# Input transfers of 112 partitions, first weights two pieces an iteration, dummy rows cleared later

## The chip, the cores and the metric

The kernel runs on one core of one Trainium2 chip. The core has five engines with queues of their own: TensorE (PE), VectorE (DVE), ScalarE (ACT), GpSimd (POOL) and SyncE (SP). SP does no arithmetic here; it issues nearly all transfers, in the order in which the program gives them. The metric is the time of one execution on the device in microseconds (us); the time before is 335.15 us, the median of three runs.

## What is computed

A recurrence with a state per head (4 batches, 8 heads, 768 steps, head size 48) produces 3072 rows of 384 numbers, and each row then goes through one of eight experts.

```python
for t in range(S):                       # per batch and head
    cur = u * k[t] (outer) v[t]
    y[t] = r[t] @ (state + cur)
    state = w[t][:, None] * state + k[t] (outer) v[t]
x = y as rows [B * S, H * D]             # 3072 x 384
logits = x @ w_gate + modality_bias[modality_id]
e = argmax(logits); g = softmax(logits)[e]
out[row] = g * (relu(x[row] @ w1[e]) @ w2[e])
```

## The kernel before, in words

The recurrence is cut into 24 units (`NU`), six chunks of 128 steps for each of four batches. A unit's r, k and w come from one host array `rkw[n]` of 128 partitions by 1536 numbers (`LIN`): columns 0 to 511 are r, 512 to 1023 k, 1024 to 1535 w. The partitions are two halves of 64, one for each head of a pair; in a half 48 rows carry numbers, and the other 16 hold zeros in r and k and ones in w, the same in every unit. So partitions 112 to 127 are constant throughout. The unit's v is a second transfer of 128 by 384 (`loadv`).

One software pipeline of iterations i = -2 to 23 runs the units. In iteration i, stage a = i + 2 does the decay scans and scales keys and rows on DVE, stage m = i + 1 makes the products of the chunk, stage z = i finishes the outputs, and stages z - 1 and z - 2 turn them into expert rows and logits. POOL works one unit ahead of a: the products of decays (`decays`, L282), of r and k (`keys`, L287) and the inner decays (`within`, L299) are made for unit i + 3. `within` writes into the input tile itself, by multiplying its r and k columns by w columns.

The input tiles are four (`ins`, `NIN` = 4), used in turn. `load(n)` (L109) fills tile n mod 4. Before the loop units 0, 1 and 2 are issued; iteration -2 issues units 3 and 4; after that iteration i issues unit i + 6, in three pieces of 256 KB, each of which waits on SP until the tile's last reader in the iteration is done. The unit's first use is in iteration n - 3, three iterations behind its issue.

Two more kinds of transfers stand in the same SP queue during the loop. `fill(j)` (L231) clears 128 of the 512 dummy rows of the DRAM buffer `xs`, with 193 KB each, in iterations `FILL` to `FILL` + 3. `w_raw` (L269) brings the first expert's weights, whose number `e0` SP reads from the tile `e0i` at iteration `EARLY`, in 16 pieces of 192 KB: eight of w1 into `raw[0]`, then eight of w2 into `raw[1]`, one an iteration. The piece order in a matrix is 2, 3, ... 7, 0, 1, since piece 0 of both tiles serves as scratch for the routing's set-up (`mf`, `bt2`) until iteration 10.

Routing of the first ten units runs in iterations 11 to 14 behind the pipeline. From iteration 15 POOL scatters the rows of the first six units into `xs`, one an iteration (`scatter`, L724). At iteration 20 (`LOAD`) SP waits for those scatters and issues the load of the first block of rows (`blk_load(0)`, L751). DVE transposes it in iterations 22 and 23 (`blk_turn`, L770), ACT and POOL split the first w1 pieces in iterations 22 and 23 (`w_split`, L276 and L277), and behind iteration 23 PE begins the experts: seven blocks of up to 512 rows with matrix products in three parts (L792 up, L813 down).

Of the kernel before, what the change touches and what calls it, by code (L numbers as in the profile page):

```python
# [17 lines left out]
B, H, S, D = 4, 8, 768, 48  # L18
P = 128
# [6 lines left out]
FC = F // P  # L26
# [37 lines left out]
SCATTER = PART[0] + 3  # L64
NEAR = 6
DRAIN = {SCATTER + 2 + n: 1 for n in range(NEAR)}
EARLY = 6
FILL = 2
NPW = 3
LOAD = SCATTER + 1 + NEAR  # L70

# [2 lines left out]
def kernel(ctx: ExitStack, tc: tile.TileContext, rkw, vt, wf, cst, mid, wg, bias, w1, w2, out):  # L74
    nc = tc.nc
# [19 lines left out]
    NIN = 4  # L95
    ins = [pa.tile([P, LIN], F32, name=f"in{i}", bufs=1) for i in range(NIN)]
# [8 lines left out]
    def pt(n, tag, sh=(P, 512)):  # L105
        T[tag, n] = (bp["s"] if tag in ("pS0", "pS1") else ps).tile(list(sh), F32, tag=tag, name=f"{tag}_{n}")
        return T[tag, n]

    def load(n, cuts=((0, LIN),)):  # L109
        for c0, c1 in cuts:  # L110
            nc.sync.dma_start(out=ins[n % NIN][:, c0:c1], in_=rkw[n, :, c0:c1])

    def loadv(n):
        nc.sync.dma_start(out=wt(n, "v", [P, DM], 4), in_=vt[n * P:(n + 1) * P, :])

    load(0, ((1024, LIN), (512, 1024)))
    wm = cp.tile([P, 512], BF16, name="wm")
    nc.vector.memset(wm, 0.0)  # L120
    cs = cp.tile([P, NCST], F32, name="cs")
    nc.sync.dma_start(out=cs[:, 0:P], in_=cst[:, 0:P])
    load(0, ((0, 512),))
    act = cp.tile([1, 1], F32, name="act")
    nc.vector.memset(act, 0.0)
# [54 lines left out]
    def early():  # L180
        nc.sync.dma_start(out=bb, in_=bass.AP(bias.tensor, bias.offset, [[0, P], [1, 2 * E]]))
        nc.sync.dma_start(out=mi, in_=mid)
# [47 lines left out]
    def fill(j):  # L230
        nc.sync.dma_start(out=xs[DUMMY + j * P:DUMMY + j * P + P, :], in_=zt)  # L231
# [36 lines left out]
    def w_raw(e, k, part, cond=None, parts=2):  # L268
        n = FC // parts  # L269
        kw = {} if cond is None else {"cond": cond}  # L270
        nc.sync.dma_start(out=raw[k][:, part * n:part * n + n, :].rearrange("p f c -> p (f c)"),
                          in_=(w1, w2)[k][ds(e, 1), :, part * n * DM:(part + 1) * n * DM].rearrange("a p c -> (a p) c"), **kw)
# [41 lines left out]
    def ok(n):  # L314
        return 0 <= n < NU
# [238 lines left out]
    def route_a(c):  # L554

        n = PART[c]
        sh = [P, n, E]
        lg = rcol(FROM[c] * E, n, E)
        if c:
            clear(c)  # L560
        nc.vector.scalar_tensor_tensor(out=lg, in0=lg, scalar=-1.0, in1=biasT[:, units(c)], op0=ALU.mult, op1=ALU.subtract)
        mx = wt(c, "mx", [P, NMOST], 1)[:, 0:n]
        nc.vector.tensor_reduce(out=mx, in_=lg, axis=AX.X, op=ALU.min)
        nc.vector.tensor_tensor(out=rcol(C_RK, n, E + 1)[:, :, 1:E + 1], in0=lg, in1=mx[:, :, None].to_broadcast(sh), op=ALU.is_equal)
        yield
        eq, flat = rcol(C_RK, n, E + 1), lambda t: t[:, 0:n].rearrange("p a b -> p (a b)")
        nc.vector.tensor_tensor_scan(out=flat(seen), data0=flat(same), data1=rcol(C_RK, n * (E + 1)), initial=0.0, op0=ALU.mult, op1=ALU.max)
        oh = T["oh", c] = wt(c, "oh", [P, NMOST, E], 2, BF16)[:, 0:n]
        nc.vector.tensor_tensor(out=oh, in0=eq[:, :, 1:E + 1], in1=seen[:, 0:n, 0:E], op=ALU.is_gt)
        yield  # L570
        nc.vector.tensor_tensor(out=lg, in0=lg, in1=mx[:, :, None].to_broadcast(sh), op=ALU.subtract)
        if c:
            with nc.allow_low_precision("whole numbers up to 10"):
                nc.vector.tensor_reduce(out=ohs, in_=T["oh", 0].rearrange("p a b -> p b a"), axis=AX.X, op=ALU.add)
        nc.gpsimd.tensor_copy(out=T["xp", c][:, :, DM + 1:DM + 2].bitcast(I32), in_=tidi[:, units(c), None])
        yield
# [168 lines left out]
    def blk_load(q, at=None):  # L745
        at = q if at is None else at
        w = width(q)
        nj, rest = divmod(w, P)
        xq, xg = x_tiles(q)
        r = nc.sync.value_load(tab[0:1, 1, ds(at, 1)], min_val=0, max_val=DUMMY)  # L750
        ins = [nc.sync.dma_start(out=xq[SQ * g:SQ * g + SQ, 0:w // SQ],  # L751
                                 in_=xs[ds(r, w), QW * g:QW * g + QW].rearrange("(t p) c -> p t c", p=SQ)) for g in range(4)]
        ins.append(nc.sync.dma_start(out=xg[:, 0:nj], in_=xs[ds(r, nj * P), DM:XW].rearrange("(j p) c -> p j c", p=P)))
        if q == 0:
            for i in ins:
                tc.add_to_no_dep_group("x0", i.ins)
        if rest:
            nc.sync.dma_start(out=xg[0:rest, nj], in_=xs[ds(r + nj * P, rest), DM:XW])
# [125 lines left out]
    setup_m()  # L884
    keys(0)
    load(1, ((1024, LIN),))
    loadv(0)
    nc.sync.dma_start(out=cs[:, P:NCST], in_=cst[:, P:NCST])
# [5 lines left out]
    def drain(n):  # L894
        for _ in range(n):
            if pend:
                n = pend.pop(0)
                if n >= NEAR:
                    place(n, 1)
                scatter(n)  # L900

    def hook_b(c):
        route_b(c)
        pend.extend(range(FROM[c], FROM[c] + PART[c]))

    for i in range(-2, NU):
        if EARLY <= i < EARLY + 2 * FC:
            if i == EARLY:
                e0 = nc.sync.value_load(e0i[0:1, 0:1], min_val=0, max_val=E - 1)
            w_raw(e0, (i - EARLY) // FC, (i - EARLY + 2) % FC, parts=FC)  # L910
        if 1 <= i < 1 + len(SETUP):
            hooks.append(SETUP[i - 1])
        if FILL <= i < FILL + BW // P:
            fill(i - FILL)
        if i == PART[0] + 1:
            ra, tb = route_a(0), table(0)
            hooks.extend([lambda: next(ra), lambda: [*ra], lambda: hook_b(0), lambda: [*tb]])
        if i == NU - 1:
            prep.close()
        att_iter(i)  # L920
        if i >= -1 and ok(i + 3):
            loadv(i + 3)
        if i == -2:
            load(3)
        if i == 0:
            early()
        if ok(i + 2 + NIN):
            load(i + 2 + NIN, ((512, 1024), (1024, LIN), (0, 512)))
        drain(DRAIN.get(i, 0))
        if i == LOAD:  # L930
            blk_load(0)
# [291 lines left out]
```

## Time and profile before

| | |
|---|---|
| median of three runs | 335.15 us (334.73 to 335.19) |
| the profiled execution | 335.87 us, its span 334.1 us |
| mean granted TensorE clock | 0.994 |
| busy share PE, DVE, ACT, POOL | 97%, 71%, 62%, 48% |
| recurrence, first to last PE work of a unit | to 121.84 us of the span |
| bytes on SP's queue | 42.09 MB |

The profile describes one execution. The span goes from the first to the last instruction. A row of a timeline gives start, duration, engine, source line, operation, destination and source, and in brackets the idle time ahead of the instruction and what ended it; without brackets the engine had no idle time worth listing there. A busy PE is not a PE at its peak.

### The profile page before, as it was taken

How to read it: one execution, taken by the hardware profiler on the slowest of the kernel's cores; microseconds unless marked ns; L12 is line 12 of the kernel's file. 1: busy time of each engine (PE TensorE's matmuls, PEld its weight loads, DVE VectorE, ACT ScalarE, POOL GpSimd, SP SyncE). 2: the span in 40 equal slices, each digit the busy share in tenths (PEclk: the TensorE clock that was granted, in tenths of full speed). 3: DMA queues.
4: the chain of work that ended last, by engine and by line, in shares of the span. 5: the costliest groups of instructions: out<-in, count | busy, mean ns of one | idle time of the engine just before them, and what ended most of it. 6: DMA issues, size and time to landing. Idle time of an engine off the chain costs nothing.

```text
span 334.1 us, 10250 instructions
## 1 busy us (share of the span) xinstructions
PE 323.0 (97%) x3915; PEld 298.8 (89%) x3915; DVE 238.4 (71%) x510; ACT 206.2 (62%) x516; POOL 158.8 (48%) x194
## 2 busy tenths in 40 slices
PE   8989899999999999999999999999999999999993
PEld 3779899999898988899889999999999988999982
DVE  7899999999999886696458858858358445815510
ACT  2478388688879994461449556956956944614420
POOL 5889999999999179136751210210220220121021
PEclk9999799999999999999999999999999999999999
DMA  7998888888894601614964800440560663210001
GB/s 220 404 307 249 248 257 267 263 261 268 264 312 154 145 4 47 144 71 169 301 195 120 254 32 0 108 177 2 114 194 2 197 141 96 94 72 22 0 32 55
DMA packets 38735, 52.31 MB, mean 157 GB/s; under 512 B 19189, under 2 KB 26133, under 8 KB 38676
## 3 DMA queue, kind: packets, MB, share of 16 engines
q1 hardware_dynamic: 35572, 42.09, 42.9%
q0 software_dynamic: 3104, 9.47, 7.6%
q8 instruction: 33, 0.54, 0.7%
q14 instruction: 26, 0.21, 0.2%
HBM read 55.43 MB, written 11.88 MB: 202 GB/s over the span
## 4 chain that ended last, share of the span: by engine, by line
issue 40%; PE 20%; POOL 8%; POOLq 2%; ACT 1%; DVE 0%; ACTq 0%
PE pS_u L792 6%; POOL out L835 6%; PE pY_d L813 3%; PE pX_d L813 2%; POOL xs L724 2%; PE pY L466 2%; POOLq L1032 2%; PE pS L415 1%; PE pY L455 1%; PE pR_x L520 1%; PE pU L435 1%; PE pR_x L321 1%; ACT dV L356 0%; POOLq L835 0%; POOLq L1010 0%
## 5 line engine op out<-in xcount | busy, mean ns | idle before, releaser
L835 POOL DMA_INDIRECT out<-ot,xg x25 | 27.4, 1096 | 132.7 <-ACT ot L834 130.6
L797 DVE SCALAR_TENSOR_TENSOR hl<-pS_u,hh 128x512 fp32r<-128x512 f32 (+2 forms) x56 | 34.6, 619 | 62.5 <-ACT hh L796 62.3
L792 PE MATMUL pS_u<-xh,wh 128*128 128x512 f32 (+2 forms) x168 | 61.6, 367 | 0.0
L796 ACT ACTIVATE hh<-pS_u 128x512 fp32r<-128x512 f32 (+2 forms) x56 | 30.3, 541 | 50.5 <-PE pS_u L792 50.5
L792 PE MATMUL pS_u<-xh,wl 128*128 128x512 f32 (+2 forms) x168 | 61.3, 365 | 0.0
L277 DVE TENSOR_TENSOR wl<-raw,wh 128x768 fp32r<-128x768 f32 x52 | 48.8, 962 | 2.3 <-ACT wh L276 1.9
L276 ACT CAST wh<-raw 128x768 fp32r<-128x768 f32 (+1 forms) x60 | 44.9, 786 | 0.0
L792 PE MATMUL pS_u<-xo,wh 128*128 128x512 f32 (+2 forms) x168 | 43.3, 365 | 0.0
L813 PE MATMUL pY_d<-wh,hh 128*128 128x384 f32 x112 | 37.8, 337 | 0.0
L813 PE MATMUL pY_d<-wh,hl 128*128 128x384 f32 x112 | 37.6, 336 | 0.0
L813 PE MATMUL pY_d<-wl,hh 128*128 128x384 f32 x112 | 37.6, 336 | 0.0
L724 POOL DMA_INDIRECT xs<-xp,posT x24 | 26.4, 1101 | 21.7 <-DVE posT L607 17.8
L335 DVE TENSOR_TENSOR_SCAN pX_s<-pw,pX_s 128x268 f32<-128x268 f32 x48 | 34.1, 711 | 1.0 <-POOL pw L282 0.7
L792 PEld LDWEIGHTS pS_u<-xh,wh 128*128 128x128 f32 x168 | 31.5, 188 | 3.2
L792 PEld LDWEIGHTS pS_u<-xh,wl 128*128 128x128 f32 x168 | 31.5, 188 | 3.1
L792 PEld LDWEIGHTS pS_u<-xo,wh 128*128 128x128 f32 x168 | 31.0, 188 | 3.6 <-DVE xo L778 0.3
L287 POOL TENSOR_TENSOR G<-in 128x512 f32<-128x512 f32 x24 | 31.1, 1294 | 4.7 <-DMA in<-rkw 4.7
L417 DVE TENSOR_TENSOR A<-pS,cs 128x1024 f32<-128x1024 f32 x24 | 29.2, 1218 | 1.0 <-PE pS L415 1.0
L415 PE MATMUL pS<-R,K 64*128 64x128 f32 x384 | 27.7, 285 | 2.2 <-DVE A L417 1.4
L356 ACT ACTIVATE dV<-v,dT 128x48 f32<-128x48 f32 x120 | 29.7, 328 | 0.0
L299 POOL TENSOR_TENSOR in<-in 128x512 f32<-128x512 f32 (+1 forms) x23 | 28.1, 1223 | 0.6
L415 PEld LDWEIGHTS pS<-R,K 64*128 64x128 f32 x384 | 24.2, 194 | 3.7 <-DVE A L417 2.2
(319 smaller groups left out, 672.5 us busy)
## 6 DMA issues: line engine op xcount, KB each, us to landing
raw<-w SPq DMA_DIRECT2D x24, 768.0 KB
in<-rkw SPq DMA_DIRECT2D x66, 256.0 KB
v<-vt SPq DMA_DIRECT2D x24, 192.0 KB
wg<-wf SPq DMA_DIRECT2D x8, 576.0 KB
raw<-w SPq DMA_DIRECT2D x16, 192.0 KB
xs<-zt SPq DMA_DIRECT2D x12, 193.0 KB
xq<-xs SPq DMA_DIRECT2D x12, 192.0 KB
xq<-xs SPq DMA_DIRECT2D x12, 144.0 KB
```

The lines of the kernel that those rows point to most:

```text
L276: nc.scalar.copy(out=wh[k][:, sl], in_=raw[k][:, sl])
L277: (eng or (nc.vector, nc.gpsimd)[k]).tensor_tensor(out=wl[k][:, sl], in0=raw[k][:, sl], in1=wh[k][:, sl].bitcast(F32), op=ALU.subtract)
L287: nc.gpsimd.tensor_tensor(out=G, in0=t[:, 0:512], in1=t[:, 512:1024], op=ALU.mult)
L335: nc.vector.tensor_tensor_scan(out=BE[:, ::step], data0=pp[:, ::step], data1=d1[:, ::step], initial=0.0, op0=ALU.mult, op1=ALU.max)
L356: nc.scalar.activation(out=dV[:, h], in_=v0[:, h], func=AF.Copy, scale=dT[:, h:h + 1])
L415: nc.tensor.matmul(out=pS[:, hh, p], lhsT=K[q, p], rhs=R[q, p], start=True, stop=True)
L724: rows_apart("xs", nc.gpsimd.indirect_dma_start(out=xs[:, :], out_offset=bass.IndirectOffsetOnAxis(ap=posT[:, n:n + 1], axis=0), in_=T["xb ...
L792: nc.tensor.matmul(out=pp, lhsT=wsrc[0][:, g, c * P:(c + 1) * P], rhs=xsrc[:, c, 0:w], start=(n == 0), stop=(n == 3 * KC - 1))
L796: nc.scalar.activation(out=hh, in_=pp, func=AF.Relu)
L797: nc.vector.scalar_tensor_tensor(out=hl, in0=pp, scalar=0.0, in1=hh.bitcast(F32), op0=ALU.max, op1=ALU.subtract)
L813: nc.tensor.matmul(out=X["y", q, j][0:r1 - r0], lhsT=hsrc[:, r0:r1], rhs=wsrc[1][:, f], start=(f == 0 and n == 0), stop=(f == FC - 1 and n ...
L835: ins = nc.gpsimd.indirect_dma_start(out=out[:, :], out_offset=bass.IndirectOffsetOnAxis(ap=xg[0:m, j, 1:2].bitcast(I32), axis=0), in_=ot[ ...
```

## The change

Three edits, all of them of what SP issues during the pipeline.

1. For units 4 and up a `load` transfers partitions 0 to 111 alone. Partitions 112 to 127 of the four tiles keep what units 0 to 3 brought.
2. `EARLY` goes from 6 to 14, and an iteration issues two weight pieces in place of one, in iterations 14 to 21; the order in a matrix becomes 0, 1, ... 7. `e0` is read at iteration 14.
3. `FILL` goes from 2 to 10: the dummy rows are cleared in iterations 10 to 13.

```diff
-EARLY = 6
-FILL = 2
+EARLY = 14
+FILL = 10
...
+    real = lambda v, n: v[0:P if n < NIN else P // 2 + D]
+
     def load(n, cuts=((0, LIN),)):
         for c0, c1 in cuts:
-            nc.sync.dma_start(out=ins[n % NIN][:, c0:c1], in_=rkw[n, :, c0:c1])
+            nc.sync.dma_start(out=real(ins[n % NIN][:, c0:c1], n), in_=real(rkw[n, :, c0:c1], n))
...
-        if EARLY <= i < EARLY + 2 * FC:
+        if EARLY <= i < EARLY + FC:
             if i == EARLY:
                 e0 = nc.sync.value_load(e0i[0:1, 0:1], min_val=0, max_val=E - 1)
-            w_raw(e0, (i - EARLY) // FC, (i - EARLY + 2) % FC, parts=FC)
+            for n in range(2 * (i - EARLY), 2 * (i - EARLY) + 2):
+                w_raw(e0, n // FC, n % FC, parts=FC)
```

## Rows read from the trace of the kernel before

**Rows 1.** The page's 40 equal slices: busy tenths of DVE and DMA, and GB/s.
```profile
DVE  7899999999999886696458858858358445815510
DMA  7998888888894601614964800440560663210001
GB/s 220 404 307 249 248 257 267 263 261 268 264 312 154 145 4 47 144 71 169 301 195 120 254 32 0 108 177 2 114 194 2 197 141 96 94 72 22 0 32 55
```

**Rows 2.** Timeline of DVE, two equal steps of neighbouring units: start, us.
```profile
53.10 0.71 DVE L335 TENSOR_TENSOR_SCAN pX_s<-pw,pX_s 128x268 f32<-128x268 f32 x1
57.60 0.71 DVE L335 TENSOR_TENSOR_SCAN pX_s<-pw,pX_s 128x268 f32<-128x268 f32 x1
```

**Rows 3.** Windows: busy us per engine with counts, PEclk, DMA share, GB/s.
```profile
14.50:19.00 4.50, 3.25 (x88) 2.93 (x86) 4.33 (x9) 3.27 (x12) 4.50 (x6) 1.00 1.05 366
28.00:32.50 4.50, 4.50 (x122) 4.32 (x121) 4.37 (x9) 3.67 (x13) 4.34 (x8) 1.00 0.92 247
55.00:59.50 4.50, 4.50 (x126) 4.32 (x124) 4.37 (x9) 3.61 (x14) 4.50 (x6) 1.00 0.83 257
95.50:100.00 4.50, 4.50 (x124) 4.29 (x122) 4.37 (x8) 4.33 (x18) 4.24 (x5) 1.00 0.97 310
```

**Rows 4.** Waits to 125 us: us in total, times, longest.
```profile
POOL G L287 <- DMA in<-rkw: 4.7, 2, 3.4
DVE pw L282 <- DMA in<-rkw: 0.7, 1, 0.7
```

**Rows 5.** Timeline of POOL: unit 1's keys, first scatter, unit 23's decays and keys.
```profile
10.12 1.30 POOL L287 TENSOR_TENSOR G<-in 128x512 f32<-128x512 f32 x1 [1.33 <-DMA in<-rkw]
...
85.00 1.21 POOL L724 DMA_INDIRECT xs<-xp,posT  x1 [0.17 <-issue]
...
104.35 0.74 POOL L282 TENSOR_TENSOR pw<-in 128x256 f32<-128x256 f32 x1
105.04 1.29 POOL L287 TENSOR_TENSOR G<-in 128x512 f32<-128x512 f32 x1
```

**Rows 6.** Timeline of SP: issues of iterations 5 to 7, 13, 17, 21.
```profile
35.87 0.43 SPq L231 DMA_DIRECT2D xs<-zt  x1
...
38.93 1.96 SPq L111 DMA_DIRECT2D in<-rkw  x3
41.95 0.36 SPq L271 DMA_DIRECT2D raw<-w  x1
...
44.11 2.13 SPq L111 DMA_DIRECT2D in<-rkw  x3
46.44 0.34 SPq L271 DMA_DIRECT2D raw<-w  x1
...
73.16 0.34 SPq L271 DMA_DIRECT2D raw<-w  x1
...
94.30 2.28 SPq L111 DMA_DIRECT2D in<-rkw  x3
...
113.58 15.70 SPq L271 DMA_DIRECT2D raw<-w  x3
```

**Rows 7.** Timelines of DVE and ACT, then the chain: the recurrence's end.
```profile
118.08 1.30 DVE L770 STREAM_TRANSPOSE xt<-xq 128x512 f32<-128x512 f32 x2
118.56 1.32 ACT L276 CAST wh<-raw 128x384 fp32r<-128x384 f32 x3
121.84 4.48 PE pS_u L792 x18
```

**Rows 8.** Timelines of PE and DVE: a stop near 36 us and what followed.
```profile
36.83 1.10 PE L466 MATMUL pY<-v,A 128*64 128x48 f32 x16 [0.97 <-issue]
40.52 1.23 DVE L417 TENSOR_TENSOR A<-pS,cs 128x1024 f32<-128x1024 f32 x1 [0.42 <-PE pS L415]
43.64 0.56 DVE L490 TENSOR_TENSOR xp<-pY,dV 128x384 f32<-128x384 f32 x1 [0.35 <-PE pY L466]
```

## The prediction

> **What bounds the kernel now.** The 40 slices come first [rows 1]: the transfers are busy to eight or nine tenths in the first twelve slices (about 100 us) and mostly idle afterwards, and all three edits act there. In the same slices DVE stands at nines. So two candidates bound this stage, the transfers and DVE, and the next views have to part them.
>
> The timeline of DVE decides it. The scan of one unit begins at 53.10 and that of the next at 57.60 [rows 2], a step of 4.50 us, and in the window of that length DVE is busy 4.37 us (the window at 55.0) [rows 3]; between the listed instructions it has no idle time. A unit therefore costs the sum of DVE's own instructions. POOL, also full in that window, works a unit ahead of DVE.
>
> The table of waits is the check: up to 125 us POOL waits for an input 2 times for 4.7 us and DVE once for 0.7 us [rows 4]. The last of these waits ends at 10.12 us, at unit 1's keys [rows 5], whose transfers were issued ahead of all that the change touches. After it nobody waits for an input tile. The transfers are busy but early. Behind 121.84 us PE runs the experts [rows 7], and it takes from the earlier stage only its starting moment.
>
> **The parts, one by one.** The sum is made against the profiled execution, 335.87 us (span 334.1), which lies 0.72 above the median of 335.15.
>
> *112 partitions.* A unit's load shrinks from 768 to 672 KB; for units 4 to 23 that is 20 x 96 KB = 1.97 MB of the 42.09 on SP's queue. Instructions and issues stay the same in number. Every engine still reads and writes 128 partitions, so no duration on DVE or POOL changes. What it saves lies beside DVE's 4.50 us a unit: 0. The trace shows no transfer of 112 rows, so its price has to be bounded: between 7/8 of a load's time and the whole of it, if rows and time don't go together. I take 7/8, and both ends are hidden, as the sum for the crowded iterations shows.
>
> *Bytes an iteration.* Before, iterations 2 to 5 issue 768 + 192 (v) + 193 (dummy rows) = 1153 KB and 6 to 17 issue 768 + 192 + 192 = 1152 KB. After, iterations 2 to 9 issue 864, 10 to 13 1057, 14 to 17 672 + 192 + 384 = 1248. From iteration 15 the scatter adds 193 KB. So the crowded stretch moves from the beginning to iterations 15 to 17: 1441 KB in 4.50 us, or 328 GB/s. The window at 95.5 moved 310 at a share of 0.97, which would be 320 at a full share, and that at 14.5 even 366 [rows 3]. By the lower figure the backlog grows by 8 GB/s x 4.5 us = 36 KB an iteration, three times: 108 KB, 0.34 us late.
>
> Against that stands the lead. Unit 23's pieces are issued from 94.30 to 96.58 [rows 6]; 768 KB at 310 GB/s take 2.5 us, so an estimate for their arrival is 99.1, and POOL first needs them at 104.35 [rows 5]. That leaves 5.2 us. A lateness of 0.34 us, or of 1.6 us if a 112-row load is no quicker than a 128-row one (4 x 96 KB more at 320 GB/s, 1.2 us), vanishes in it: 0. Without the lead POOL, then DVE, would be late by just that much.
>
> *Weights.* The 16 pieces and their 16 issues stay. SP gets 0.34 us more of issuing in each of iterations 14 to 21 and 0.34 less in 6 to 13 [rows 6]. The register read of the expert's number moves along: at iteration 6 SP needed 1.06 us from the end of the load's issue (38.93 + 1.96) to the first piece (41.95), at iteration 7 0.20, so the read costs 0.86. At iteration 14 the v of unit 17 and the load of unit 20 stand behind 0.86 + 0.34 = 1.20 us more on SP, and both have a lead of three iterations. 0.
>
> Are the pieces early enough? ACT splits the first three of w1 at 118.56 [rows 7]. They are issued in iterations 14 and 15, before 94.30. The last two pieces of w2 are issued at iteration 21, where the last piece is issued now, at 113.58 behind the load of the first block; the order now makes them the last needed ones as well. The first block's load has one more 192 KB piece ahead of it, from iteration 20; with the queue at about 320 GB/s that is 0.6 us, beside a wait of SP for the sixth scatter that it does not touch. DVE's transpose at 118.08 shows no idle time ahead of it. 0.
>
> *Dummy rows.* Four issues of about 0.43 us, the last at 35.87 [rows 6], leave iterations 2 to 5 and stand in 10 to 13. The scatters write the same buffer and must stay behind them; the first starts at 85.00 [rows 5], and iteration 13 issues at about 73.16 [rows 6]: 11.8 us of cover. If that were gone the first scatter would wait and take the sixth, and with it the first block's load, along. 0.
>
> *One stop that might go.* At 36.83 PE resumes half of a loop after 0.97 us in which the profile finds nothing that it waited for [rows 8], while zero rows, v and inputs are in flight. PE is then behind, and DVE, the bound, loses 0.42 us at 40.52 and 0.35 at 43.64: 0.77 us. This is the only place between 11 and 113 us where DVE loses more than a quarter of a microsecond. If PE's own instructions came late behind the data, iterations 2 to 9 with a quarter fewer bytes would remove the stop; if not, it stays. Bounds: -0.77 and 0. I take 0, for two reasons. The windows at 14.5 and 95.5 with shares of 1.05 and 0.97 show no such stop (366 and 310 GB/s against 247 at 28.0) [rows 3], so load alone does not make it. And the profiled execution is 0.72 us longer than the median, close to the 0.77: the timed runs may well not have the stop at all.
>
> The Trainium skill ("Runtime: NRT & Kernel Launch", section "Instruction fetch mechanics") says that instructions are brought in blocks ahead of their execution and that crossing from block to block is mostly hidden. By that rule the stop has another cause, the change cannot remove it, and the time is that of no change; without the rule the gain of 0.77 stands. No row here shows PE's blocks arriving, so it stays open.
>
> **Sum.** 335.87 + 0 for the profiled execution, less the 0.72 by which that one lies above the median: 335.15, rounded to 335.1. About 0.2% (0.67 us) is what a measurement of this kernel can tell from no change.
>
> **Rivals.**
> *A, the forecast: hidden, 335.1 us.* For it: DVE's step of 4.50 and the missing waits behind 10.12. Against: the share of the transfers near 0.9, and the stop.
>
> *B, the stop is in every execution and goes.* For it: the zero rows are issued at 35.87, just ahead. Against: the two fuller windows without one. 335.15 - 0.77 = 334.4, hardly over the bound.
>
> *C, slower: iterations 14 to 17 become the bound.* The place is POOL's first use of units 20 to 23. The four iterations issue 4 x 1248 + 3 x 193 = 5571 KB, 5.70 MB, in 18.0 us; to use up the 5.2 us of lead they would have to take 23.2 us, so the mechanism decides below 246 GB/s at a full share. The nearest bad row is the window at 28, 247 GB/s at a share of 0.92, or 268 at a full one: 21.3 us, 3.3 late, still covered. Were 112-row transfers to run less well and the rate fall to 235, the four iterations would take 24.3 us, and 1.1 us would come through to POOL and DVE: 336.2. The stop of PE would cost the same order if it moved here: 335.15 + 0.77 = 335.9.
>
> *D, the change saves no transfer time at all* (a 112-row load as long as a 128-row one): 1.6 us late at most, still covered, 335.1; it is counted with A.
>
> **Chances.** A with D 0.60, B 0.26, C 0.14. Of A I give 0.05 to faster and 0.03 to slower, for the spread of the runs (334.73 to 335.19) around the bound; of B 0.20 is faster and 0.06 the same, since 0.77 is close to 0.67; of C 0.13 slower and 0.01 the same. Faster 0.25, same 0.59, slower 0.16. The range goes from 334.2, B with a little more, to 336.1, nearly all of C; A alone would be 334.8 to 335.4.
>
> **What would show it.** Right: DVE's step stays at 4.50 us and its first expert work, PE's start at 121.84, moves by less than half a microsecond; the share falls to about 0.65 in iterations 2 to 9 and reaches about 1 in 15 to 17; no wait of POOL or DVE for an input behind 11 us. B shows as a missing stop near 36 us and PE's start 0.77 earlier, C as waits of POOL's keys for an input between 90 and 106 us. The forecast is wrong if DVE's step changes where no wait is listed, or if the time moves behind 121.84 us while that moment stays.

## The result, and the profile after

The changed kernel is slower: 338.14 us (median of 20 runs, 335.10 to 342.58) against 335.00 (20 runs, 334.31 to 335.95). The ratio is 1.0074, 95% interval 1.0052 to 1.0095; it leaves out the four longest runs, 341.97 to 342.58. The profiled execution took 336.33 us, span 334.4, so it is one of the changed kernel's shortest, 1.8 us below its median. Read alone it shows nearly nothing of the loss; that is why the experiments below take several profiles.

The page of the changed kernel, the slices that answer to [rows 1]:

```profile
DVE  7999999999999786696458858858358445815510
DMA  7998766788996511614964810540550673310001
GB/s 239 345 262 235 214 194 187 226 252 231 302 314 209 130 45 47 144 71 169 302 193 120 246 39 0 109 175 2 119 189 2 187 150 96 94 73 21 0 32 55
```

The third slice of the transfers is full, as before, but it moves 262 GB/s where it moved 307. The windows answer to [rows 3]: busy time of the engines with counts, granted clock, DMA share, GB/s.

```profile
14.50:19.00 4.50, 3.25 (x86) 3.06 (x88) 4.24 (x9) 3.27 (x12) 4.50 (x6) 1.00 1.08 267
28.00:32.50 4.50, 4.50 (x126) 4.34 (x122) 4.37 (x8) 3.06 (x12) 4.34 (x8) 1.00 0.78 233
55.00:59.50 4.50, 4.50 (x121) 4.32 (x120) 4.37 (x9) 3.73 (x14) 4.50 (x7) 1.00 0.69 199
95.50:100.00 4.50, 3.58 (x96) 3.28 (x92) 4.37 (x9) 3.40 (x13) 4.23 (x5) 1.00 1.07 301
```

At 14.5 a share of 1.08 now goes with 267 GB/s where 1.05 went with 366: the transfer engines are as busy and carry a quarter less. The trace has a time for every packet: one of 2 KB, the size of an input's row, took 127 ns in that window (the median) where it took 87 before, and in the one at 95.5 it took 114 where it took 84; at 28.0 and 55.0, where the changed kernel's share is below 0.8, it took 84 in both kernels. In the window at 95.5 they are full, and PE is busy 3.58 us of 4.50 in place of 4.50. The waits for inputs [rows 4] and DVE's step [rows 2] are as they were:

```profile
POOL G L289 <- DMA in<-rkw: 4.0, 2, 3.1
DVE pw L284 <- DMA in<-rkw: 0.7, 1, 0.7
```

Timeline of DVE, two neighbouring units and the first block's transpose [rows 2, 7]:

```profile
51.87 0.71 DVE L337 TENSOR_TENSOR_SCAN pX_s<-pw,pX_s 128x268 f32<-128x268 f32 x1
...
56.36 0.71 DVE L337 TENSOR_TENSOR_SCAN pX_s<-pw,pX_s 128x268 f32<-128x268 f32 x1
...
118.27 1.29 DVE L772 STREAM_TRANSPOSE xt<-xq 128x512 f32<-128x512 f32 x2
```

The step is 4.49 us, and the first block is there when DVE comes to it. So neither the inputs nor the first block are late in this profile; what changed is what a full share carries, and that PE has holes.

### The profile page after: what moved, and what is told of

Its sections match the earlier page's. It is cut to its first block, busy times and chain, and to the rows that moved or that the text cites. A ratio compares the mean times of both kernels' runs of the same rounds, so it can differ in the third digit from the quotient of the medians.

```text
span 334.4 us, 10251 instructions
## 1 busy us (share of the span) xinstructions
PE 322.6 (96%) x3915; PEld 298.1 (89%) x3915; DVE 238.3 (71%) x510; ACT 206.7 (62%) x516; POOL 158.9 (48%) x194
## 4 chain that ended last, share of the span: by engine, by line
issue 40%; PE 29%; POOL 8%; POOLq 2%; ACT 1%; DVE 0%; ACTq 0%
PE pS_u L794 6%; POOL out L837 6%; PE pY L468 4%; PE pS L417 3%; PE pY L457 3%; PE pY_d L815 3%; PE pX_d L815 2%; POOL xs L726 2%; PE pR_x L323 2%; PE pU L437 2%; PE pR_x L522 2%; POOLq L1035 2%; ACT dV L358 0%; POOLq L837 0%; POOLq L1013 0%
## 5 line engine op out<-in xcount | busy, mean ns | idle before, releaser
L837 POOL DMA_INDIRECT out<-ot,xg x25 | 27.4, 1095 | 132.8 <-ACT ot L836 127.5
L815 PE MATMUL pY_d<-wh,hl 128*128 128x384 f32 x112 | 37.6, 336 | 0.0
L815 PE MATMUL pY_d<-wl,hh 128*128 128x384 f32 x112 | 37.6, 336 | 0.0
L358 ACT ACTIVATE dV<-v,dT 128x48 f32<-128x48 f32 x120 | 29.7, 326 | 0.0
L419 DVE TENSOR_TENSOR A<-pS,cs 128x1024 f32<-128x1024 f32 x24 | 29.2, 1216 | 0.6 <-PE pS L417 0.6
L417 PE MATMUL pS<-R,K 64*128 64x128 f32 x384 | 27.1, 280 | 1.6 <-DVE A L419 1.3
L468 PE MATMUL pY<-v,A 128*64 128x48 f32 x736 | 26.0, 222 | 1.1 <-issue 0.9
```

Of the source, the lines that this page charges most:

```text
L417: nc.tensor.matmul(out=pS[:, hh, p], lhsT=K[q, p], rhs=R[q, p], start=True, stop=True)
L468: nc.tensor.matmul(out=pY[q:q + 64, h * D:(h + 1) * D], lhsT=A[:, hh, p, q:q + 64], rhs=v[:, h * D:(h + 1) * D], start=(first(z) and h == ...
L815: nc.tensor.matmul(out=X["y", q, j][0:r1 - r0], lhsT=hsrc[:, r0:r1], rhs=wsrc[1][:, f], start=(f == 0 and n == 0), stop=(f == FC - 1 and n ...
L837: ins = nc.gpsimd.indirect_dma_start(out=out[:, :], out_offset=bass.IndirectOffsetOnAxis(ap=xg[0:m, j, 1:2].bitcast(I32), axis=0), in_=ot[ ...
```

## The experiments

Every time is compared with the kernel before, run beside it on the same chip; its median was 334.8 to 337.7 us on the chips used, so times of different chips don't compare. A ratio is given with its 95% interval. Theory 1 was that 112-row transfers use the transfer engines badly; theory 2 that the rows are innocent and the crowding of the weights does it.

**Loads alone.**

```diff
+    for n in range(12):                     # a phase; seven phases, rows r0 to r1
+        for c in (512, 1024, 0):
+            nc.sync.dma_start(out=big[r0:r1, ...], in_=rkw[n, r0:r1, c:c + 512])
```

> Leaves out the whole computation and writes zeros: seven phases of loads alone, 12 units of three pieces each, with rows 0-127 (twice), 0-111, 0-63 and 64-111 as two transfers, 0-95, 0-95 and 96-111 as two, 0-111 again. Theory 1 (a 112-row transfer uses the transfer engines badly): 128 rows run at 350 GB/s or more, about 27 us a phase of 9.44 MB, and 112 rows at 265 GB/s or less, so a phase of 8.26 MB takes 30 us or more, longer than the one of 128. Theory 2 (the rows are innocent, the crowding of weights is the cause): 112 rows run at the rate of 128, within 5%, about 24 us.

The timeline of DVE has one small copy at each phase's end, which waits for all its loads; the bracket is the phase's time. The order is 128, 128, 112, 64 + 48, 96, 96 + 16, 112 rows.

```profile
29.02 0.17 DVE L90 COPY got<-big 128x12 f32<-128x12 f32 x1 [27.66 <-DMA big<-rkw]
...
57.23 0.17 DVE L90 COPY got<-big 128x12 f32<-128x12 f32 x1 [27.70 <-DMA big<-rkw]
...
89.89 0.17 DVE L90 COPY got<-big 128x12 f32<-128x12 f32 x1 [32.15 <-DMA big<-rkw]
...
133.80 0.17 DVE L90 COPY got<-big 128x12 f32<-128x12 f32 x1 [43.41 <-DMA big<-rkw]
...
163.96 0.18 DVE L90 COPY got<-big 128x12 f32<-128x12 f32 x1 [29.72 <-DMA big<-rkw]
...
200.43 0.17 DVE L90 COPY got<-big 128x12 f32<-128x12 f32 x1 [35.97 <-DMA big<-rkw]
```

128 rows take 27.7 us for 9.44 MB (341 GB/s); 112 rows take 32.15 us for 8.26 MB (257 GB/s), and 32.32 in the last phase, whose copy is not listed here. An eighth fewer bytes cost 16% more time (32.15 / 27.7). The windows of the first phase and of the first one with 112 rows, with the share of the transfer engines and the GB/s at the end, tell whether some of the transfer engines stood idle:

```profile
1.50:29.00 27.50, 0.00 (x0) 0.00 (x0) 1.00 0.96 343
57.60:89.80 32.20, 0.12 (x1) 0.00 (x0) 1.00 0.96 257
```

The share is 0.96 in both, so idle engines are not the difference. By it a row of 2 KB holds one of the 16 transfer engines for 0.96 x 16 x 27.5 us / 4608 rows = 92 ns in the first and 0.96 x 16 x 32.2 / 4032 = 123 ns in the other. Theory 1 holds for the transfers.

**The rows alone, and the queue alone.**

```diff
 EARLY = 6, FILL = 2, one piece an iteration      # rows_only: the loads of the change
...
+    real = lambda v, n: v[0:P if True else P // 2 + D]    # queue_only: 128 rows, the rest of the change
```

> The kernel before with 112 rows from the fifth unit on, weights and zero rows where they were. Theory 1: slower than before by 1 to 5 us and scattered, since with one piece an iteration and slow 112-row loads every iteration is near a full share. Theory 2: the same as before within 0.2%.

> The change with all loads of 128 rows: weights two an iteration from 14 on, zero rows in 10 to 13. Theory 1: within 0.5 us of before, runs within 1.5 us of each other. Theory 2: as slow and as scattered as the change, 337 to 340 us, as 1344 KB an iteration are issued in 14 to 17.

Rows alone: ratio 1.0079 (1.0043 to 1.0115). Queue alone: 1.0005 (0.9980 to 1.0030). All of the loss needs the rows; moving weights and zero rows costs nothing that can be told. Theory 2 falls. The runs of the queue alone lie further apart than expected (335.29 to 339.46 us without one longer one, against 335.36 to 338.20 of the kernel before).

**The change once more.**

> The changed kernel once more, for a second profile and its spread: about 338 us, 335 to 342. Theory 1: where it is longer than before, PE has stops in which nothing is listed that it waits for, at shares of the transfers near 1 with under 270 GB/s, in iterations 0 to 3 and 14 to 18. Theory 2: the stops stand in 14 to 18 alone.

Ratio 1.0101 (1.0054 to 1.0148); its profiled execution took 338.24 us, its span was 336.3. The chain of waits of it: start, duration, what.

```profile
94.87 0.94 PE pY L468 x26
95.81 1.54 issue
97.34 0.38 PE pY L468 x5
...
102.18 0.28 PE pS L417 x2
102.46 0.52 issue
102.98 1.16 PE pS L417 x14
...
107.72 0.50 PE pS L417 x7
108.22 0.65 issue
108.87 0.72 PE pS L417 x9
109.59 0.56 PE pR_x L323 x16
...
114.13 0.56 PE pR_x L323 x16
```

Two things are to be seen. PE stops in the middle of loops with nothing listed that it waits for, three times, 2.71 us together. And where it doesn't stop, a unit takes PE 4.54 us (109.59 to 114.13): DVE's 4.50 is not alone, PE has no time to spare with which to make up a stop. What it may wait for can be found in the view of the transfers, first from 94.5 to 95.8, then from 95.95 to 97.34 us (packets, MB, share of the transfer engines):

```profile
q1 hardware_dynamic: 246, 0.35, 97.5%
q8 instruction: 1, 0.02, 6.3%
...
q1 hardware_dynamic: 202, 0.33, 101.6%
q0 software_dynamic: 6, 0.03, 6.4%
```

Queue 8 brings blocks of 16 KB, one in about 5 us here and in about 23 us among the experts; PE begins on average some 250 products and weight loads between two of them in either stage, so they are taken for PE's instructions. The trace gives that packet's time as 94.6 to 95.9; PE's records end at 95.81 and go on at 97.34. The fifteen profiles of whole kernels have 27 stops of PE of 0.4 us and more between 11 and 125 us for which nothing is listed that PE waits for. In all 27 PE resumes 1.25 to 1.62 us behind the end of such a packet, [rows 8] among them, though the packets come only every 5 us or so. That is a match in time, not a run in which the blocks alone were moved; what makes a block late was not seen either.

The change's stops of half a microsecond and more stand at 20 to 22 and at 97 to 109 us. In the 4.5 us ahead of them the transfers have a share of 0.99 to 1.08 and move 249 to 321 GB/s, with one exception: ahead of the stop that ends at 108.87 the share is 0.41. So most of the stops stand where the transfers are full, as theory 1 has it, but with more than the 270 GB/s that it named for the late ones.

**What makes the rows dear.**

```diff
+    in_=rkw[n, 0:112, c:c + 512].rearrange("(a b) c -> a b c", b=8)     # 14 groups of 8 rows
```

> Leaves out the whole computation and writes zeros: seven phases of loads alone, 12 units of three pieces, with rows 0-127; 0-119; 0-111 with the source written as 14 groups of 8 rows; 16-127 plain; 0-63; 0-95 with the source as 12 groups of 8; 0-111 plain. Theory 1a (the rows are slow where a transfer engine gets other than eight of them): the phases with 8 rows a group take what 128 rows take, 27.7 us (27 to 29), and 16-127 plain takes 32 like 0-111. Theory 1b (any transfer of fewer rows has dearer rows): the grouped ones take 30 us and more too.

The same copies as above, for 128; 120; 112 in 14 groups of 8; 16 to 127 plain; 64; and 96 rows in 12 groups of 8:

```profile
28.71 0.17 DVE L92 COPY got<-big 128x12 f32<-128x12 f32 x1 [27.35 <-DMA big<-rkw]
66.82 0.17 DVE L92 COPY got<-big 128x12 f32<-128x12 f32 x1 [37.60 <-DMA big<-rkw]
98.06 0.17 DVE L92 COPY got<-big 128x12 f32<-128x12 f32 x1 [30.72 <-DMA big<-rkw]
130.58 0.17 DVE L92 COPY got<-big 128x12 f32<-128x12 f32 x1 [32.02 <-DMA big<-rkw]
156.58 0.17 DVE L92 COPY got<-big 128x12 f32<-128x12 f32 x1 [25.49 <-DMA big<-rkw]
184.32 0.17 DVE L92 COPY got<-big 128x12 f32<-128x12 f32 x1 [27.23 <-DMA big<-rkw]
```

Theory 1a (eight rows an engine is all that counts) fails: 96 rows in groups cost what 128 cost, but 112 in groups 30.7 and 120 even 37.6. That a group went to one engine is not shown: the trace has 16 packets under 512 B to each transfer in groups, as to one of 128 rows, and 15 to one of 120. Theory 1b fails at the 96. What stands is the table: no shorter form is cheaper in proportion, and half the rows cost 93% of the time (25.49 / 27.35). The Trainium skill ("DMA: Bandwidth & Descriptors", "The descriptor swizzle") says that in a transfer of 128 partitions each engine writes one port of SBUF. No run here shows ports, and why the rows are dear stays open.

> The changed kernel with the same 112 rows, the source written as 14 groups of 8. Theory 1a: back at the kernel before, within 0.5 us, or with the weights' crowding at most 1 us slower, and no share above 1.05 in 20 to 28 us. Theory 1b: as slow as the change, 2 to 3 us more than before.

The changed kernel with these groups: 1.0101 (1.0080 to 1.0123), as slow as the change. Its profile has PE stops that end at 21.3 (1.38 us) and 97.6 (1.46 us).

**Full transfers without short rows.**

```diff
-            w_raw(e0, (i - EARLY) // FC, (i - EARLY + 2) % FC, parts=FC)
+            for n in (i - EARLY, i - EARLY - 1, i - EARLY - 2):
+                if n == i - EARLY or 0 <= n and i < 18:
+                    w_raw(e0, n // FC, (n + 2) % FC, parts=FC)
```

> The kernel before with loads of 128 rows, and up to two weight pieces an iteration brought a second time in iterations 7 to 17 (21 x 192 KB, 1536 KB an iteration, 350 GB/s with 341 measured for loads alone). Theory 1 (full transfers, by whatever cause, make PE stop for its own instructions): 1 to 5 us slower than before and scattered, PE stops of half a microsecond and more with nothing listed, POOL waits for no input or only late. Rival (112-row transfers do it by themselves): within 0.5 us of before, or slower by waits of POOL's keys for inputs.

Ratio 1.0022 (1.0005 to 1.0038), a median 0.65 us longer, a fifth of the change's 3.14: the sign is theory 1's, but the size lies below its 1 to 5 us and is not clear of the rival's 0.5. Its profile has the stops, three of them:

```profile
85.86 0.63 PE L455 MATMUL pY<-SPb,R 128*64 128x96 f32 x9 [0.50 <-issue]
...
96.59 0.38 PE L466 MATMUL pY<-v,A 128*64 128x48 f32 x6 [0.64 <-issue]
...
102.22 1.16 PE L415 MATMUL pS<-R,K 64*128 64x128 f32 x14 [0.52 <-issue]
```

Load makes such stops with 128 rows too (ahead of the last one the transfers moved 376 GB/s), but 4 MB more of it costs far less than 2 MB less in short rows.

**Two tries at a faster kernel.** The pieces of the weights later, and k and w of a unit as one transfer:

```diff
+            for n in (range(k, k + 1) if k < 4 else range(4 * k - 12, 4 * k - 8)):   # k = i - 14, to i = 20
+                w_raw(e0, n // FC, n % FC, parts=FC)
...
-                load(i + 2 + NIN, ((512, 1024), (1024, LIN), (0, 512)))
+                load(i + 2 + NIN, ((512, LIN), (0, 512)))
```

> The kernel before, 128 rows, zero rows early as before, one weight piece an iteration in 14 to 17 and four in each of 18 to 20, when no inputs are loaded any more; 6 to 13 then issue 960 KB in place of 1152. Theory 1: fewer stops of PE, 0 to 1 us faster than before. Rival (crowding in 18 to 20 delays scatters and the first block): 0.5 to 2 us slower, DVE waits for the first block at the transpose.

> The kernel before, 128 rows, k and w of a unit as one transfer of 4 KB rows in place of two of 2 KB. If PE's instruction blocks wait behind many small packets, fewer and longer ones change how often PE stops: 0 to 1 us faster than before where longer rows move quicker, 0 to 1 us slower where a block waits for a longer packet; the same within 0.2% if the blocks don't mind 128-row traffic at all.

Later weights: 1.0019 (1.0003 to 1.0036). Its profile is the shortest seen (334.74 us, experts from 120.5), and DVE waits 1.02 us for the first block in it, as the rival had it, but the runs fall into eight near 334.8 and four from 336.2 to 337.1. Two pieces: 1.0004 (0.9980 to 1.0029). Neither beats the kernel before.

**Where the loss comes through.**

```diff
+    real = lambda v, n: v[0:P if n < NIN or n >= 12 else P // 2 + D]   # rows_early, old queue
+    real = lambda v, n: v[0:P if n < 12 else P // 2 + D]               # rows_late, old queue; rows_late_queue, new queue
```

> 112 rows for units 4 to 11 alone, 128 for the rest; weights and zero rows as before the change. Theory 2a (PE has no time to spare from about 80 us to the end of the recurrence, so only what stops it there comes through): within 0.7 us of before, since PE's stops near 20 to 30 us are taken up while DVE sets the step. Theory 2b (every stop comes through, wherever): 1 to 2 us slower, as much as rows late.

> 112 rows for units 12 to 23 alone, the rest as before the change. Theory 2a: most of the change's loss, 1 to 3 us slower than before, PE stops behind 75 us about 1.5 us behind the end of a 16 KB instruction block. Theory 2b: 1 to 2 us, half of the loss of all units.

Early rows: 1.0052 (1.0022 to 1.0082). Late rows: 1.0006 (0.9976 to 1.0037). That is the reverse of theory 2a, by which the early stops would be taken up, and 2b fails as well. In the early profile PE stops 1.02 us at 21.2, POOL waits 0.38 us for an input at 15.6 and DVE 0.56 for the routing bias at 23.6. With the late rows and the new queue together:

> The changed kernel with 128 rows up to unit 11 and 112 from unit 12 on; weights two pieces an iteration in 14 to 21, zero rows in 10 to 13. Theory 3a (the loss has two places: the first units, whose inputs and PE blocks are late behind 112-row loads, and the last ones, where 112 rows and two pieces an iteration together stop PE): 0.2 to 0.7% slower than before, PE stops behind 90 us. Theory 3b (the first units alone): within 0.2% of before.

1.0052 (1.0025 to 1.0078): late rows cost when the weights come two at a time beside them, which goes with the 2 KB packets' times above, dear where the transfers are full. But this interval and that of the late rows with the old queue overlap, on two chips, and the rows alone cost 0.8% with the old queue; so both places count, as theory 3a has it, and whether their parts, 0.5% each, add up to the change's 0.7 to 1.0% is not shown. The profile of this run did not catch its loss in that place: it has no stop of PE behind 90 us, against the expectation. Its 337.35 us come from the experts' stage, where PE waits 1.78 us for a tile of DVE's (hl) up to 167.36 us; the second profile of the kernel before has 1.13 us of the same wait. Nor does the profile of the rows alone (336.51 us) have a late stop.

> The changed kernel, another profile on this chip. Theory 3a: DVE's product of the fourth unit at 25.7 to 27.1 us, and 22 us or more from its product of unit 19 to the first expert work, where the kernel before has 21.2; PE stops behind 90 us.

> As the run ahead of it: what differs between the two is chance, and the longer one has the more stops of PE, each some 1.4 us behind the end of a 16 KB instruction block.

> The kernel before, a second profile beside those: 21.2 to 21.6 us from DVE's product of unit 19 to the first expert work, and no stop of PE over 1 us behind 90 us.

These took 340.61, 339.16 and 337.58 us. The expectations hold but for two points: the fourth unit's product stands at 28.29 us in the first, where 25.7 to 27.1 was expected, and the longer of the two profiles of the change has no more stops of 0.4 us than the other, two each, but longer ones. Four stretches of every profile, in us: to DVE's product (L417 or L419) of unit 3, from there to that of unit 19, from there to the first expert product on PE, and the rest of the span:

| profile | to unit 3 | to unit 19 | to the experts | rest |
|---|---|---|---|---|
| before | 26.24 | 74.39 | 21.15 | 212.3 |
| before, second | 26.75 | 73.81 | 21.32 | 213.9 |
| the queue alone | 25.89 | 73.43 | 21.53 | 213.2 |
| rows alone | 26.74 | 73.46 | 21.35 | 213.2 |
| the change | 25.95 | 73.43 | 22.59 | 212.4 |
| the change, second | 25.72 | 74.00 | 23.65 | 212.9 |
| the change, third | 28.29 | 74.03 | 23.44 | 213.0 |
| the change, fourth | 27.08 | 73.98 | 23.27 | 213.1 |
| rows in groups | 25.97 | 73.98 | 22.59 | 212.3 |
| before with extra pieces | 25.68 | 73.45 | 23.40 | 212.4 |

In all four profiles of the change the third stretch, up to the experts, is 1.3 to 2.5 us longer than in the two of before; the stops of 0.25 us and more behind 95 us, with nothing listed that PE waits for, come to 0.92, 2.71, 1.32 and 1.16 us in them, so the sizes are alike, though not one for one. The loss of the timed runs is 2.5 to 3.4 us (0.7 to 1.0%). The first stretch is longer in two of the four, by up to 2.0; the windows of the third profile show what happens there:

```profile
20.00:21.00 1.00, 0.78 (x25) 0.71 (x24) 1.00 (x5) 0.44 (x3) 1.00 (x2) 1.00 1.06 233
21.00:22.00 1.00, 0.11 (x3) 0.11 (x4) 0.96 (x3) 0.63 (x3) 1.00 (x2) 0.61 1.06 242
22.00:23.00 1.00, 1.00 (x17) 1.00 (x18) 1.00 (x2) 0.33 (x2) 0.46 (x1) 0.50 1.05 267
...
25.00:26.00 1.00, 1.00 (x20) 0.91 (x18) 0.35 (x1) 0.00 (x0) 1.00 (x1) 0.50 1.06 260
...
28.00:30.00 2.00, 2.00 (x60) 1.83 (x59) 1.71 (x4) 1.07 (x6) 0.31 (x2) 0.99 0.93 270
```

PE is busy 0.11 us in the microsecond of its stop (1.10 us, for which nothing is listed), then the granted clock is 0.50, that is 1.2 of 2.4 GHz, until 28 us; DVE, busy 0.35 at 25, now waits for PE. That the stop makes the clock fall is not shown: in the fourth profile it falls at 19.67 us, ahead of a stop of 0.69 us that ends at 20.99, and in the kernel before with extra pieces it is 0.50 from 19.69 to 23.10 us without any such stop near. There the first stretch is no longer for it (25.68); in the two profiles of the change with 6.8 us at half clock it is 27.08 and 28.29.

The rest of the span varies by chip and run from 212.3 to 216.1, in the kernel before as well (212.3, 213.9); the program is the same there, and no profile ties it to the change. What the longest runs of the change (over 341 us) lose, and where, was not profiled and stays open.

## Why the prediction was wrong

*The step that failed* is the one on 112 partitions: "between 7/8 of a load's time and the whole of it ... I take 7/8, and both ends are hidden". By itself the load takes 1.16 of the whole, outside both bounds. The upper bound had no row behind it: that fewer bytes cannot take longer was assumed, and the loads alone refute it. With rows and queue parted, the loss stays with the rows (1.0079 against 1.0005).

*The cover was looked up for the wrong user.* The sum for iterations 15 to 17 asked whether inputs have enough lead, and they have: no profile of the change lists a wait of POOL's keys or of DVE for an input behind 28 us. But the packets taken for PE's instructions go through the same transfer engines (queue 8 has 6.3% of them in the view above), and "vanishes in it: 0" is true of inputs alone. The late stops, at 97 to 109 us, stand where the sum saw only a lateness that is covered. The sign that the prediction named for itself, PE's start on the experts within half a microsecond of 121.84, holds in the first profile (121.97) and fails in the other three (123.37 to 125.76).

*The bound was half read.* DVE's step of 4.50 us was measured rightly and is the same where PE doesn't stop. PE's own unit is 4.54 us at the end; in the window that the prediction used PE was busy 4.50 of 4.50 [rows 3]. With two engines at the limit a stop of either comes through, so the stretch up to the experts costs 1.3 to 2.5 us, where the prediction priced a stop by the waits of DVE, 0.77. By the table even the stop near 36 us cost more: the second stretch is 74.39 us with it and 73.43 with the queue alone, whose profile has no such stop.

*The stop near 36 us* [rows 8] was read as a possible gain. It is absent in the first profile of the change, as rival B wanted, and others came in its stead. But B had it in every execution, and the second profile of the kernel before has two others in its place:

```profile
26.79 0.17 PE L520 MATMUL pR_x<-cs,xT 128*64 128x8 f32 x1 [0.77 <-issue]
...
42.92 0.55 PE L466 MATMUL pY<-v,A 128*64 128x48 f32 x10 [1.12 <-issue]
```

So where the stops fall is chance in either kernel; behind 90 us the two profiles of the kernel before have none and each of the four of the change has one or more. Their likely cause, late instructions, was put aside for two windows of higher share without a stop. Two windows were too few: with extra pieces PE stops at 376 GB/s and a share of 1.03. The prediction set beside it the rule of the Trainium skill ("Runtime: NRT & Kernel Launch", "Instruction fetch mechanics") that crossing from block to block is mostly hidden. As a count that agrees here, 27 stops at 329 blocks; that a stop must then have another cause does not follow, and if the match in time is the cause, what is left unhidden is up to 1.54 us a stop.

*Rival C* had the place and the sign, iterations 14 to 17 at the limit, and a rate (246 GB/s) close to what the short rows give alone (257). Its mechanism, POOL late for inputs, did not occur; its last sentence, that PE's stop might move here, names what the profiles show, priced at 335.9. It was given 0.14, with 336.1 as its time.

*What held:* weights and zero rows at 0 with loads of 128 rows (the queue alone, 1.0005), the transpose without a wait, the share of 0.69 in the middle and 1.07 in the crowded window.

## What to carry to other kernels

Before bytes are saved by transferring fewer partitions, measure that shape by itself: here 112 rows took 16% longer than 128, and the saving turned into a loss. When transfers become fuller, ask for the lead of everything that uses them, the engines' instructions among it, and look for the engine with the second longest step: without slack on PE, its late stops reached the end here. A profile is one draw: here it lay 1.8 us below the median of the kernel that it stands for.

## What the runs showed of the hardware

Loads of 36 pieces with 2 KB rows took, by rows: 128: 27.4 to 27.7 us; 120: 37.6; 112: 32.2; 16 to 127: 32.0; 112 in 14 groups: 30.7; 96: 29.7; 96 in 12 groups: 27.2; 64: 25.5; 64 + 48 as two: 43.4; 96 + 16 as two: 36.0. In the kernel a 2 KB packet took 127 ns in place of 87 where the transfers were full (14.5 to 19 us) and 84 in both kernels where they were not (55 to 59.5). In 27 stops of PE with nothing listed, of 0.4 to 1.54 us, PE went on 1.25 to 1.62 us behind the end of a 16 KB packet of queue 8. After one stop of 1.10 us PE ran at half clock for about 6 us, after the one near 36 us [rows 8] for 3.3 (to 40.11); behind stops of 1.54 and 1.12 us the granted clock stayed at 1.00.
